# Pinned, delayed transfers, quartered weight loads and a second buffer for the doubles in a fused attention, mixture-of-experts and Fourier-mixing kernel

## The chip, the cores and the metric

The program runs on one core of one Trainium2 chip. The metric is the device time of one execution in microseconds (us); lower is better. A core has five engines that run side by side, each through its own list of instructions in order: TensorE (PE, with PEld for its weight loads), VectorE (DVE), ScalarE (ACT), GpSimd (POOL) and SyncE (SP), which here does little but issue transfers. They wait for each other through semaphores. A transfer is issued by an engine and then carried out by the core's DMA engines.

## The reference

Three stages follow one another for 8 batches of 576 tokens with 512 channels: attention against keys and values that are averaged over 8 tokens, a mixture of 8 experts with a routing that carries over along the tokens, and a Fourier transform over both axes with a normalization and a two-layer network behind it. Cut to what is computed:

```python
def _attn_ref(q, k, v):                        # (8, 8, 576, 64) each
    k_p = k.reshape(B, H, Sp, pool, D).mean(axis=3)          # Sp = 72
    v_p = v.reshape(B, H, Sp, pool, D).mean(axis=3)
    scores = scale * np.matmul(q, k_p.transpose(0, 1, 3, 2))
    scores = scores - np.max(scores, axis=-1, keepdims=True)
    attn = np.exp(scores)
    attn = attn / (np.sum(attn, axis=-1, keepdims=True) + 1e-09)
    return np.matmul(attn, v_p)

def _moe_ref(x, w_gate, w_local, w1, w2):      # w1 (8, 512, 1024), w2 (8, 1024, 512)
    ...                                        # per token: e = fresh argmax, or the token before's
    h = np.maximum(x[b, s] @ w1[e], 0.0)
    out[b, s] = p[e] * (h @ w2[e])

def _moe2_ref(x, w_ch1, w_ch2):                # the weights are doubles
    mixed = np.real(np.fft.fft(np.fft.fft(x, axis=1), axis=2))
    u = x + mixed
    un = (u - mu) / np.sqrt(var + 1e-06)
    return u + np.maximum(un @ w_ch1, 0.0) @ w_ch2
```

## The kernel before

The program has a first part (attention and experts, batch by batch) and a second part (the Fourier mixing and its network), with a loop between them (L1112) that runs once for each further expert that a batch needs; with these data it runs zero times.

**First part.** `moe(b)` multiplies the 576 tokens of batch b by the two weight matrices of one expert, w1 (L460, L461) and w2 (L483, L490). The weights are split into two half-precision parts, so each product is three matmuls. `moe` is a generator of 34 steps. After each step the main loop (L1101 to L1106) advances `chain()`, which runs the attention of the batches to come a fixed number of its own steps further, and `fill()`, which takes a step from `todo`, a list of small jobs. So during moe(b) the program holds the second half of the attention of batch b+1, the first half of that of batch b+2, the load of the weights of b+1 and their splitting, and the decoding of the doubles of the second part.

**One attention tile.** A batch has five tiles. Each goes through `load_q` (L212), `att_A` (L225: PE transposes q), `att_B` (L237: PE scores at L239, softmax on DVE and ACT, the result in two half-precision parts `ehl` at L260 and L261, then a DMA transpose of `ehl` into the tile `ET` at L263), `att_D` (L280: PE multiplies ET by the averaged values at L290, into `xhl`), and `att_L` (PE at L308, the routing). When all five are through, the expert is known, and the program reads its number into a register of SP (L326).

**Weights.** `load_w` (L390) loads one matrix of an expert, 2 MB, in two transfers of 1 MB (L395): w1 into the buffer `wr0`, w2 into `wr1`. In the trace both are `wr`. `max_parts` (L400) takes the largest weight (DVE L405), spreads it over the partitions by an all-reduce on POOL (`across`, L139, tile `wm`), and makes a scale of it (DVE L131). `split_parts` (L422) then makes the two parts: ACT scales (L431) and rounds (L432), POOL subtracts (L433, tiles `w0l` for w1 and `w1l` for w2). `wr0` and `wr1` have one buffer each, so the w2 of batch b+1 can be loaded only after POOL has written the `w1l` of batch b. POOL also averages the keys and values (L170 to L172).

**Doubles.** The weights of the second part come as 64-bit numbers and are decoded in 32 pieces of 512 KB (`load_f64` L620 into the tile `dd`, ACT L635 into `et`, DVE L637 to L641 into `dt`, store at L644). `dd` has one buffer, so each load of a piece waits for the piece before to be decoded (L641).

**What sets the order.** Nearly all transfers are issued by SP, one after the other in SP's list. The program's text gives a first order, but a scheduler of the framework places each instruction by its own priorities; only an instruction marked with `tc.keep_in_program_order` keeps its place in the text. In the first part nothing is so marked before. A transfer that must wait (for its data or for its buffer) holds up every transfer behind it in SP's list.

## Time and profile before

| what | value |
| --- | --- |
| three timed runs | 1580.87, 1561.38, 1581.09 us; median 1580.87 |
| the profiled execution | 1555.29 us |
| its span, from the first to the last instruction | 1553.5 us |
| busy in the span: PE, DVE, ACT, POOL | 1360.3 (88%), 1044.4 (67%), 569.3 (37%), 383.5 us (25%) |
| start, attention of batch 0 | 0 to 76.7 us |
| moe(0) to moe(6) begin on PE at | 76.7, 156.5, 237.7, 322.4, 401.1, 489.1, 565.0 us |
| the last matmul of moe(6) ends | 626.6 us |
| PE waits at the loop | to 647.6 us |
| second part | 647.6 to 1553.5 us |

All times in the rows are of the profiled execution, in us from the start of its span. The profile groups instructions by source line, engine, operation and tiles, written out<-in. A wait in it is the idle time of an engine ahead of an instruction, together with what ended it.

### The profile page before, as it was taken

What the parts mean: (1) busy time and instruction counts of PE and PEld (TensorE: products, weight loads), DVE (VectorE), ACT (ScalarE), POOL (GpSimd) and SP (SyncE); (2) the same over time, 40 slices, a digit from 0 to 9 for tenths busy, and PEclk for the clock granted to TensorE, in tenths of its full rate; (3) what the DMA queues carried; (4) which work ended last, traced back from release to release, by engine and by line L of the source; (5) the groups of instructions that cost most, each with busy time, mean ns of one, the idle gap of its engine ahead of it and who ended that gap; (6) DMA issues with size and microseconds to landing.
All of it is one profiled execution on the core that took longest, in us unless ns stands there. A gap on an engine that the chain in (4) does not pass through costs nothing.

```text
span 1553.5 us, 24994 instructions
## 1 busy us (share of the span) xinstructions
PE 1360.3 (88%) x9674; PEld 842.6 (54%) x9674; DVE 1044.4 (67%) x2197; ACT 569.3 (37%) x1071; POOL 383.5 (25%) x465
## 2 busy tenths in 40 slices
PE   3588888787888898487699999999999999999997
PEld 2454444454444454243566666666666766666663
DVE  5797877776686788258487687565667676576432
ACT  1365556464547475335332221222222221222110
POOL 3562926253446141336201010010101001000000
PEclk8589999898999899679699999999999999999999
DMA  8659897787796767335536053161605235243010
GB/s 164 177 143 254 188 243 178 227 159 236 149 286 163 201 160 194 104 100 147 92 109 131 20 102 62 59 105 49 108 8 113 51 82 82 78 109 75 12 44 28
DMA packets 245954, 193.98 MB, mean 125 GB/s; under 512 B 185254, under 2 KB 191270, under 8 KB 244806
## 3 DMA queue, kind: packets, MB, share of 16 engines
q1 hardware_dynamic: 230198, 172.21, 46.7%
q0 software_dynamic: 10272, 10.41, 2.9%
q10 hardware_dynamic: 5360, 9.70, 1.8%
q8 instruction: 78, 1.28, 0.3%
q14 instruction: 46, 0.38, 0.1%
HBM read 111.83 MB, written 47.37 MB: 102 GB/s over the span
## 4 chain that ended last, share of the span: by engine, by line
PE 47%; DMA 5%; DVE 3%; issue 1%; SPq 1%; ACT 1%; POOL 0%; DVEq 0%; ACTq 0%
PE mm L920 18%; PE s L987 11%; PE et L987 6%; PE hg L987 5%; DMA out_dram<-c 2%; PE mm L460 2%; PE a L870 2%; PE a L869 1%; PE a L877 1%; DMA xhl<-un 1%; DMA dd<-fw_dram 1%; PE a L758 1%; SPq L993 0%; SPq L817 0%; DMA ab<-un 0%
## 5 line engine op out<-in xcount | busy, mean ns | idle before, releaser
L925 DVE TENSOR_TENSOR c<-mm,c 128x512 f32<-128x512 f32 x180 | 122.7, 686 | 151.0 <-PE mm L920 146.4
L460 PE MATMUL mm<-xhl,w0h 128*128 128x512 f16 x512 | 172.9, 406 | 32.9 <-POOLq L1112 21.0
L920 PEld LDWEIGHTS <-wr 128*128 128x128 f16 x1728 | 168.9, 98 | 60.1 <-issue 22.1
L772 POOL DMA_DIRECT2D yb<-y_dram x42 | 26.8, 655 | 475.4 <-DVE pt L822 391.6
L920 PEld LDWEIGHTS <-ex 128*128 128x128 f16 x1296 | 126.8, 99 | 25.3 <-issue 5.1
L987 PEld LDWEIGHTS <-hl 128*128 128x128 f16 x864 | 83.8, 98 | 94.9 <-issue 1.6
L987 PEld LDWEIGHTS <-hh 128*128 128x128 f16 x864 | 84.6, 98 | 86.7 <-issue 0.5
L920 PE MATMUL mm<-xhl,wr 128*128 128x256 f16 x864 | 107.5, 275 | 22.0 <-DMA xhl<-un 22.0
L930 ACT COPY c<-mm 128x512 f32<-128x512 f32 x72 | 41.4, 584 | 185.7 <-PE mm L920 161.4
L920 PE MATMUL mm<-xhl,ex 128*128 128x256 f16 x864 | 108.4, 277 | 0.0
L936 ACT ACTIVATE hl<-c 128x512 f16<-128x512 f32 x72 | 45.3, 629 | 163.2 <-DVE c L925 163.2
L460 PE MATMUL mm<-xhl,w0l 128*128 128x512 f16 x256 | 103.2, 403 | 0.0
L490 PE MATMUL mm<-w1h,hh 128*128 128x512 f16 x256 | 99.7, 389 | 0.5 <-DVE hl L465 0.5
L460 PEld LDWEIGHTS <-w0h 128*128 128x128 f16 x512 | 50.8, 102 | 89.5 <-issue 39.3
L490 PE MATMUL mm<-w1h,hl 128*128 128x512 f16 x256 | 99.0, 387 | 0.0
L490 PE MATMUL mm<-w1l,hh 128*128 128x512 f16 x256 | 98.9, 386 | 0.0
L936 ACT ACTIVATE hh<-c 128x512 f16<-128x512 f32 x72 | 44.9, 630 | 119.2 <-DVE c L925 119.1
L431 ACT ACTIVATE wr<-wr,wscale 128x512 f32<-128x512 f32 x120 | 82.0, 718 | 10.6 <-DVE wscale L135 8.0
L461 PE MATMUL hg<-xhl,w0h 128*128 128x64 f16 x512 | 84.5, 197 | 0.0
L433 POOL TENSOR_TENSOR w0l<-wr,w0h 128x512 f16<-128x512 f32 x56 | 63.3, 1155 | 69.4 <-ACT wr L431 23.0
L405 DVE TENSOR_REDUCE wmax<-wr 128x1 f32<-128x1024 f32 x64 | 76.6, 1210 | 4.2 <-DMA wr<-in_moe_w_dram 4.2
L490 PEld LDWEIGHTS <-hh 128*128 128x128 f16 x512 | 48.9, 99 | 53.4 <-issue 4.2
(296 smaller groups left out, 3138.3 us busy)
## 6 DMA issues: line engine op xcount, KB each, us to landing
wr<-in_moe_w_dram SPq DMA_DIRECT2D x32, 1024.0 KB
dd<-in_moe_w_ch_dram SPq DMA_DIRECT2D x32, 512.0 KB
kraw<-in_k_dram SPq DMA_DIRECT2D x8, 1152.0 KB
vraw<-in_v_dram SPq DMA_DIRECT2D x8, 1152.0 KB
xs_dram<-xhl SPq DMA_DIRECT2D x8, 1152.0 KB
y_dram<-y ACTq DMA_DIRECT2D x32, 256.0 KB
fw_dram<-dt SPq DMA_DIRECT2D x32, 256.0 KB
u_dram<-yb SPq DMA_DIRECT2D x32, 256.0 KB
```

Source lines behind the costliest of these rows:

```text
L405: V.tensor_reduce(out=m[:, c:c + 1], in_=tc_, axis=AX.X, op=ALU.max, apply_absolute_value=True)
L431: S.activation(out=t[:, sl], in_=t[:, sl], func=ACTF.Copy, scale=s)
L433: G.tensor_tensor(out=l[:, sl], in0=t[:, sl], in1=h[:, sl], op=ALU.subtract)
L460: P.matmul(po, lhsT=ww[:, c], rhs=x[:, j, kk, 64:576], start=st, stop=sp)
L461: P.matmul(go, lhsT=ww[:, c], rhs=x[:, j, kk, 0:64], start=st, stop=sp)
L490: P.matmul(po, lhsT=hx[:, f, c0:c0 + n], rhs=ww[:, 512 * f:512 * f + 512], start=(f == 0 and t == 0), stop=(f == 7 and t == 2))
L870: P.matmul(o, lhsT=fd[2][gw, n, :M], rhs=tabs[nm][gw, 1, i], start=False, stop=True)
L920: P.matmul(o[:, q], lhsT=fw1[n][:, w, kk, f], rhs=unT[b][x][:, u, kk, :], start=(kk == 0 and i == 0), stop=(kk == 1 and i == 2))
L925: TT(out=c, in0=x, in1=y, op=ALU.add)
L930: S.copy(out=c, in_=o)
L936: S.activation(out=d[0], in_=c, func=ACTF.Relu)
L987: P.matmul(acc[i], lhsT=h[:, x, hf, q, 128 * i:128 * i + 128], rhs=fw2[w][hf][:, 512 * f:512 * f + 512], start=(f == 0 and hf == 0 and n = ...
```

## The change

It has five pieces, all in the first part.

1. **Transposes.** `att_B` no longer issues the transpose of `ehl` at once. It puts it on a list `later`, which is worked off at the end of the next step of the chain (`do_later`), and the transpose is pinned to that place of the program.
2. **q.** `load_q` within `attention` goes on the same list, and its transfers are pinned.
3. **Weights.** `load_w` becomes a generator of four pinned transfers of 512 KB. `moe` puts the generator on a list `loads`, and `steps` issues one quarter after each step of `moe`.
4. **Doubles.** `dd` has two buffers in the first part. Two pieces are loaded at the start, a piece fetches the one after the next, and its load and its store are pinned and stand one step later.
5. **Housekeeping.** A table of `count_extras` reuses a tile. In the loop (`in_order`) nothing is pinned.

The loads of the keys and values and the read of the expert's number are not pinned.

```diff
-    BUFS = {"xhl": 2, ..., "c": 5}
+    BUFS = {"xhl": 2, ..., "c": 5, "dd": 2}
+    def pin(ins):
+        return ins if in_order else tc.keep_in_program_order(ins)
+    in_order = []
+    later = []
+    def do_later():
+        for f in later:
+            f()
+        later.clear()
@@ load_q
-            D.dma_start(out=t, in_=q[b, :, s0:s0 + 128, :].rearrange("h s d -> s h d"))
+            pin(D.dma_start(out=t, in_=q[b, :, s0:s0 + 128, :].rearrange("h s d -> s h d")))
@@ att_B
-        D.dma_start_transpose(out=ET[b, i][:, :, :, :n]..., in_=hl[:n]...)
+        et = ET[b, i]
+        later.append(lambda: pin(D.dma_start_transpose(out=et[:, :, :, :n]..., in_=hl[:n]...)))
@@ load_w
-        kc = 4 if which == 0 else 8
-        for h in range(2):
-            n = kc // 2
-            D.dma_start(out=tile_[:, 2048 * h:2048 * h + 2048]...,
-                        in_=src[bass.ds(e, 1), 128 * n * h:128 * n * (h + 1)]...)
+        n = (1, 2)[which]
         wr[key, which] = tile_
+        for h in range(4):
+            pin(D.dma_start(out=tile_[:, 1024 * h:1024 * h + 1024]...,
+                            in_=src[bass.ds(e, 1), 128 * n * h:128 * n * (h + 1)]...))
+            yield
@@ moe, beside
-                load_w(b + 1, ereg[b + 1], 0, wtile([128, 4096], F32, "wr0"))
+                loads.append(load_w(b + 1, ereg[b + 1], 0, wtile([128, 4096], F32, "wr0")))
...
-                load_w(b + 1, ereg[b + 1], 1, wtile([128, 4096], F32, "wr1"))
+                loads.append(load_w(b + 1, ereg[b + 1], 1, wtile([128, 4096], F32, "wr1")))
+        def steps(g):
+            for _ in g:
+                if loads and next(loads[0], "end") == "end":
+                    loads.pop(0)
+                yield
-            yield from moe1_f(b, f, hh, hl, hg)
+            yield from steps(moe1_f(b, f, hh, hl, hg))
-            yield from moe2_t(b, i, hh, hl, c, done)
+            yield from steps(moe2_t(b, i, hh, hl, c, done))
+        for g in loads:
+            drain(g)
@@ attention
-                    load_q(b + (r + 3) // 5, (r + 3) % 5)
+                    later.append(lambda: load_q(b + (r + 3) // 5, (r + 3) % 5))
...
                 yield
+                do_later()
@@ decode_parts
-        load_f64(c + 1)
-        yield
-        D.dma_start(out=fw_dram[c // 2, ...], in_=t.bitcast(F32))
+        yield
+        load_f64(c + 2)
+        pin(D.dma_start(out=fw_dram[c // 2, ...], in_=t.bitcast(F32)))
         yield
```

Three places of the order, before and of the change. The first is SP's list in moe(5): ET are the transposed attention weights, made of ehl0 or ehl1 in turn, wr0 and wr1 the buffers for w1 and w2. Before:

```order
L326 TENSOR_LOAD fe_i_5666
L326 ISA x2
L395 ISA
L395 DMA wr0_5724<-in_moe_w1_dram 128x2x1024
L263 DMA_TRANSPOSE ET_5481<-ehl1_99 128x16x128
L395 ISA
L395 DMA wr0_5724<-in_moe_w1_dram 128x2x1024
L395 ISA
L395 DMA wr1_5890<-in_moe_w2_dram 128x4x512
L395 ISA
L395 DMA wr1_5890<-in_moe_w2_dram 128x4x512
L263 DMA_TRANSPOSE ET_5603<-ehl0_98 128x16x128
```

And in the changed kernel (L279 is the transpose, L412 the weight load):

```order
L412 DMA wr0_5750<-in_moe_w1_dram 128x1024
L412 ISA
L412 DMA wr0_5750<-in_moe_w1_dram 128x1024
L279 DMA_TRANSPOSE ET_5629<-ehl0_98 128x16x128
L412 ISA
L412 DMA wr0_5750<-in_moe_w1_dram 128x1024
L279 DMA_TRANSPOSE ET_5802<-ehl1_99 128x16x128
L412 ISA
L412 DMA wr0_5750<-in_moe_w1_dram 128x1024
L412 ISA
L412 DMA wr1_5916<-in_moe_w2_dram 128x2x512
```

The fourth transpose (from ehl0) stood behind all of w1 and both halves of w2; it now stands behind two quarters of w1, and the fifth behind three. The last quarter of w1 stands behind the fifth transpose. In moe(1) to moe(6) of the changed kernel all five transposes stand ahead of the first quarter of wr1.

The second place is POOL's list in moe(4): the all-reduces (L139) of the weights' maxima (wm0 for w1, wm1 for w2) and of the values' (vmax), the averaging (L172) and the splitting (L433). Before:

```order
L139 ISA
L139 ISA wm0_5103<-am_5101 128x1
L139 ISA vmax_5328<-am_5325 128x1
L172 ISA
L172 TENSOR_TENSOR kp_5340<-kraw_5181 72x128
L433 TENSOR_TENSOR w0l_5229<-wr0_4761,w0h_5228 128x512 x3
L139 ISA
L139 ISA wm1_5395<-am_5393 128x1
L433 ISA
L433 TENSOR_TENSOR w0l_5229<-wr0_4761,w0h_5228 128x512 x5
```

And in the changed kernel (L154, L187 and L450 are the same three lines):

```order
L154 ISA
L154 ISA wm0_5129<-am_5127 128x1
L187 ISA
L187 TENSOR_TENSOR kp_5363<-kraw_5207 72x128
L450 TENSOR_TENSOR w0l_5253<-wr0_4783,w0h_5252 128x512 x3
L154 ISA
L154 ISA vmax_5354<-am_5351 128x1
L450 ISA
L450 TENSOR_TENSOR w0l_5253<-wr0_4783,w0h_5252 128x512 x5
L187 TENSOR_TENSOR kp_5363<-kraw_5207 72x128
L154 ISA
L154 ISA wm1_5420<-am_5418 128x1
```

Here two visits to the all-reduce have become three, since vmax no longer goes with wm0. In moe(0) to moe(6) there were 1, 3, 3, 3, 2, 2, 3 visits and are now 2, 2, 3, 2, 3, 2, 3; there are as many in all of the first part.

The third place is PE's list around the last att_D (L290) of moe(3), where a1 is its result and vs are the averaged values. Before:

```order
L461 MATMUL hg_3704<-xhl_2623,w0h_3302 128x64
L460 LDWEIGHTS w0l_3303
L460 MATMUL mm_4149<-xhl_2623,w0l_3303 128x512
L290 LDWEIGHTS vs_3580
L290 MATMUL a1_4097<-ET_3850,vs_3580 64x128
```

And in the changed kernel (L507 is a matmul with w2, L306 is att_D):

```order
L507 MATMUL mm_4220<-w1h_3735,hh_3719 128x512
L507 LDWEIGHTS hh_3719
L507 MATMUL mm_4220<-w1l_3736,hh_3719 128x512
L306 LDWEIGHTS vs_3598
L306 MATMUL a1_4119<-ET_3868,vs_3598 64x128
```

Counted by the wide matmuls (512 columns) of moe(3), the last att_D stood behind 90 of the 96 of the first product, and now stands behind 116, 20 into the second product.

## Rows read from the trace of the kernel before

**Rows 1.** Windows by stage: stretch, length, busy time by engine, PEclk, DMA share, GB/s.

```profile
76.70:565.00 488.30, 411.54 (x3383) 227.36 (x3383) 372.15 (x857) 269.48 (x520) 227.98 (x259) 0.93 0.79 199
626.60:647.60 21.00, 0.04 (x3) 0.02 (x2) 4.77 (x20) 6.99 (x16) 6.34 (x7) 0.56 0.22 67
790.00:1553.50 763.50, 747.79 (x4932) 493.48 (x4929) 484.37 (x940) 180.19 (x318) 39.00 (x68) 1.00 0.32 70
```

**Rows 2.** Waits of PE, 76.7 to 565: us in total, times, longest.

```profile
PE a L290 <- DMA ET<-ehl: 41.6, 14, 8.4
PE mm L460 <- DVE y L506: 7.8, 2, 6.0
```

**Rows 3.** Timeline of PE: start, us, instruction, [idle before <- releaser].

```profile
285.85 1.50 PE L290 MATMUL a<-ET,vs 72*64 72x128 f16 x24 [8.44 <-DMA ET<-ehl]
...
322.36 0.39 PE L460 MATMUL mm<-xhl,w0h 128*128 128x512 f16 x1
...
362.94 1.28 PE L290 MATMUL a<-ET,vs 72*64 72x128 f16 x20 [7.43 <-DMA ET<-ehl]
...
411.97 1.03 PE L460 MATMUL mm<-xhl,w0h 128*128 128x512 f16 x2 [6.01 <-DVE y L506]
...
520.19 1.50 PE L290 MATMUL a<-ET,vs 72*64 72x128 f16 x24 [7.30 <-DMA ET<-ehl]
```

**Rows 4.** Timeline of SP's transfers, around the last stall and one piece of doubles.

```profile
496.39 4.80 SPq L263 DMA_TRANSPOSE ET<-ehl  x1
501.41 9.80 SPq L395 DMA_DIRECT2D wr<-in_moe_w_dram  x3
511.32 6.71 SPq L263 DMA_TRANSPOSE ET<-ehl  x1
...
396.42 0.34 SPq L620 DMA_DIRECT2D dd<-in_moe_w_ch_dram  x1
```

**Rows 5.** Waits of SP's queue, 76.7 to 565.

```profile
SPq L620 <- DVE dt L641: 69.8, 16, 10.2
SPq L263 <- DVE ehl L261: 34.5, 8, 8.2
...
SPq L395 <- POOL w1l L433: 25.8, 5, 7.8
```

**Rows 6.** Windows around the three long stalls, columns as in Rows 1.

```profile
280.80:291.00 10.20, 4.99 (x43) 2.94 (x44) 8.00 (x20) 1.48 (x3) 0.38 (x1) 0.50 1.03 252
359.30:369.50 10.20, 6.57 (x50) 3.48 (x51) 1.45 (x3) 2.32 (x4) 1.60 (x2) 0.50 0.99 287
516.30:526.50 10.20, 6.31 (x52) 3.50 (x53) 4.13 (x9) 1.87 (x3) 0.00 (x0) 0.50 0.65 172
```

**Rows 7.** Waits of ACT for doubles, 76.7 to 565.

```profile
ACT et L635 <- DMA dd<-in_moe_w_ch_dram: 27.2, 13, 5.1
```

**Rows 8.** Timeline of ACT: the decoding of the piece issued at 396.42.

```profile
400.96 0.64 ACT L635 ACTIVATE et<-dd 128x512 f32<-128x512 f32 x1 [2.87 <-DMA dd<-in_moe_w_ch_dram]
```

**Rows 9.** Timeline of POOL: splits and all-reduces.

```profile
314.42 5.60 POOL L433 TENSOR_TENSOR w0l<-wr,w0h 128x512 f16<-128x512 f32 x5 [7.32 <-ACT cm L560]
...
370.10 0.38 POOL L139 PARTITION_ALL_REDUCE wm<-am  x1 [9.12 <-issue]
...
407.86 0.38 POOL L139 PARTITION_ALL_REDUCE wm<-am  x1 [5.97 <-issue]
...
645.99 1.14 POOL L433 TENSOR_TENSOR w1l<-wr,w1h 128x512 f16<-128x512 f32 x1 [7.53 <-issue]
```

**Rows 10.** Timeline of DVE: the fifth tile's ehl and the maximum of w1, moe(3).

```profile
349.09 0.76 DVE L261 TENSOR_TENSOR ehl<-sc,ehl 128x576 f16<-128x576 f32 x1 [1.07 <-ACT ehl L260]
...
357.05 0.15 DVE L147 TENSOR_REDUCE am<-wmax 128x1 f32<-128x4 f32 x1
```

**Rows 11.** Window of two weight halves in flight, columns as in Rows 1.

```profile
348.00:352.00 4.00, 4.00 (x41) 2.18 (x40) 2.73 (x5) 1.65 (x3) 4.00 (x4) 1.00 0.97 394
```

More of the change, by code (lines that the diff above doesn't have):

```diff
@@ L528, in moe @@
         todo.append(w2s)
+        loads = []
         at = {}
@@ L1041, in count_extras @@
     def count_extras():
-        oh = pool["sb"].tile([128, B, 5, 8], F32, tag="x_oh", name="x_oh", bufs=1)
+        oh = mt([128, B, 5, 8], F32, "E")
         cnt = small([128, B, 8], F32, "x_cnt")
@@ L1083, in attention_moe_fourier_kernel @@
         advance(a, done_steps[0] + 1)
-    load_w(0, ereg[0], 0, wtile([128, 4096], F32, "wr0"))
-    load_w(0, ereg[0], 1, wtile([128, 4096], F32, "wr1"))
+    drain(load_w(0, ereg[0], 0, wtile([128, 4096], F32, "wr0")))
+    drain(load_w(0, ereg[0], 1, wtile([128, 4096], F32, "wr1")))
     advance(a, done_steps[0] + WAIT_W)
```

24 lines of the change are left out of this document (13 added, 11 removed).

## The prediction
> **What bounds the kernel now.** I read the windows by stage first. From 790 us on, PE is busy 747.79 of 763.50 us at full clock [rows 1]; the change moves next to nothing there, so that part is taken as it is. In the stretch of moe(0) to moe(5), 76.70 to 565.00, PE is busy 411.54 of 488.30 us, so 76.8 us are lost there, with the DMA engines busy 0.79 of the time. From 626.60 to 647.60 PE does nothing: POOL's last split of w1l begins at 645.99 [rows 1, 9]. That tail waits for POOL's work, which the change leaves as it is.
>
> Next, PE's waits in the first stretch. The largest is att_D's for its transposed weights: 41.6 us in 14 waits [rows 2]. PE's timeline shows that three of them make up more than half: 8.44, 7.43 and 7.30 us, together 23.2 us, ending at 285.85, 362.94 and 520.19 [rows 3]. SP's timeline says why, at the last of them: a transpose at 496.39, then three halves of weights from 501.41 on, which hold SP for 9.80 us, and only at 511.32 the transpose that PE waits for [rows 4]. Among the three halves are those of w2, which wait until POOL has done with w1l: SP waits so 25.8 us in 5 waits, up to 7.8 us each [rows 5]. So the transposes are late because they stand behind loads whose buffer isn't free. The order shows the same in moe(2), moe(3) and moe(5), the three places of the long stalls.
>
> Around each long stall lies a stretch at a granted clock of 0.50, the lower of the two levels (1.2 GHz) [rows 6]. PE is busy there 4.99 + 6.57 + 6.31 = 17.9 us, half of which, 8.9 us, is lost to the clock.
>
> **The change, part by part.**
>
> *Transposes pinned, one step later, and weights in quarters.* These belong together: no transpose stands behind a wr1 quarter of its batch any more, but behind at most three quarters of wr0. And att_D itself stands later on PE (in moe(3) behind 116 wide matmuls rather than 90), so a transpose has more time. I take the three long waits as gone: −23.2 us [rows 3], and with them the low clock: −8.9 us [rows 6]. The eleven shorter waits sum to 41.6 − 23.2 = 18.4 us [rows 2]. Between nothing and all of it I take half, −9.2 us: a transpose still queues behind other data (one held SP 4.80 us with no wait for a buffer [rows 4]), and it is issued a step later.
>
> *Quarters as such.* Two halves in flight together move 394 GB/s, 0.97 of the DMA engines [rows 11]. There are now 24 more transfers in moe(0) to moe(5). Issued at 0.34 us each [rows 4], that is 8 us on SP, which waits 69.8 + 34.5 + 25.8 = 130 us in three lines alone [rows 5]; so I count it as nothing. If SP had no such waits, it would be the 8 us. What a small transfer costs by itself has a bound in the doubles, 512 KB too: issued at 396.42, used at 400.96, 4.5 us [rows 4, 8], against 512 KB / 394 GB/s = 1.3 us in the flow [rows 11]. So it is between 0 and 3.2 us, and since quarters are queued one behind another, I take 0 and keep 3.2 for a rival.
>
> *q.* Its loads were ordered by the scheduler and are now at a fixed place. PE's waits name none of it among the large ones; I take nothing.
>
> *Doubles in two buffers.* SP waits 69.8 us for the buffer in 16 waits [rows 5], and ACT 27.2 us for the data [rows 7]. But PE feels this only where ACT or DVE is late for it. The nearest row is PE's wait for y (L506), 7.8 us in 2 waits, of which 6.01 us at 411.97 [rows 2, 3], 11 us behind a decode that had waited 2.87 us for its data [rows 8]. The bounds are 0 and −7.8; I take −2, since DVE's own length of work there doesn't change.
>
> *What comes next: POOL.* So far the gain is 23.2 + 8.9 + 9.2 + 2 = 43.3 us, 7.2 us for each of six batches. If PE is done sooner, the next moe wants its w0l sooner. Now POOL ends w0l at 314.42 + 5.60 = 320.02, and moe(3) starts at 322.36 [rows 3, 9]: a slack of 2.3 us. POOL pays for every visit to the all-reduce: 5.97 us idle before it at 407.86 and 7.53 us before the next split, at 645.99 [rows 9]. In all there are as many visits as before, but moe(2) and moe(4) have three of them, moe(4) one more than it had. There I let POOL take back what goes beyond the slack: 7.2 − 2.3 = 4.9 us, twice, +9.8 us. The bounds are 0 and the same in all six batches, +29.4.
>
> **The sum** is −43.3 + 9.8 = −33.5 us. It is made against the profiled execution, 1555.29 us. The three runs shown are 25.6, 6.1 and 25.8 above it, 19.2 in the mean, which I add: 1574.5 (their median is 6.4 above that). 1574.5 − 33.5 = 1541.0 us.
>
> **The rivals.**
>
> *POOL takes over in every batch.* For it: the slack of 2.3 us, and the switches of 6 and 7.5 us. Against it: POOL is busy only 227.98 of 488.30 us [rows 1]. Then the gain is 43.3 − 29.4 = 14 us, with 8 to 22 around it: 1552 to 1566.
>
> *All waits go.* The two-buffer decode and the fixed order take all of 41.6 + 8.9 + 7.8 = 58.3 us, and POOL gives nothing back, because its inputs come sooner too: 1516; up to 1528 if a part of the short waits stays.
>
> *Slower: the last quarter of w0.* It is pinned behind the fifth transpose, and so behind the fifth ehl, which in moe(3) is done at 349.09 + 0.76 = 349.85 [rows 10]. A transpose held SP 4.80 to 6.71 us [rows 4], and the quarter lands 1.3 to 4.5 us later: at 356 to 361. The maximum is now complete at 357.05 + 0.15 = 357.2 [rows 10], and POOL's all-reduce follows at 370.10; if its switch of 5.97 us begins only with the data, the maximum could come until 364.1 [rows 9]. From there on, 6.9 us later than now, each us would move w0l and the next moe. To undo the gain (33.5 / 6 = 5.6 us for each batch) and add 27 us in all (4.5 for each), it would have to come 5.6 + 4.5 + 2.3 = 12.4 us later still in every batch; that gives 1574.5 + 27 = 1601. Against it: the quarters start early in a batch, and the bounds above end before 364.1.
>
> *The quarters cost by themselves.* At 3.2 us for each of 24 more transfers, one behind another, that is 77 us; with the gain of 33.5, +43: 1618. Against it, the window with two transfers in flight runs at 0.97 [rows 11], and several are queued most of the time.
> The Trainium skill, page "DMA: Bandwidth & Descriptors", section "Bandwidth", says the same in general: transfers should be batched to at least 1 MiB to come near the peak; and its section "Anatomy of one DMA" puts the fixed cost of a transfer at about 2.0 us. By that page, as an estimate, 24 more would cost 48 us if none overlapped, and 1 MB transfers ought to be left whole. The trace agrees that one 512 KB transfer alone is far from the rate of two large ones, but it shows no serial chain of them.
>
> *Nothing happens.* The order shows that the transposes do move, so this can be only if the short waits grow as the long ones go. It is the lower end of the POOL case.
>
> **How the numbers follow.** Chances: forecast, gain of 22 to 46 (1528 to 1552), 0.50; POOL takes over (1552 to 1566), 0.24; all waits go (1516 to 1528, with the noise of the runs to 1508), 0.15; w0's last quarter, 0.07; cost of the quarters, 0.04. Two per cent, about what a measurement of this kernel can tell from no change, is 31.5 us of 1574.5. The forecast lies almost on this bound, so I divide it, 0.28 faster and 0.22 the same. Faster: 0.28 + 0.15 = 0.43. The same: 0.22 + 0.24 + 0.03 (a mild case of the late quarter) = 0.49. Slower: 0.04 + 0.04 = 0.08. The range goes from 1508, where no wait is left and the runs lie 8 us low, to 1568, the end of the POOL case. The forecast's own range is 1528 to 1552.
>
> **What the profile of the changed kernel would show.** Right: PE's waits of att_D for ET fall from 41.6 to about 9 us with none over 4; no stretch at 0.50 between 237 and 565; SP's transfers in moe(2), moe(3) and moe(5) show the transposes ahead of the wr1 quarters; moe(6) starts near 531 rather than 565; PE still waits about 21 us at the loop. For POOL: a wait of L477 (L460 before) for w0l in moe(3) or moe(5) of about 5 us. Wrong: waits for w0l in all batches (POOL took over); SP held at the last wr0 quarter, and the all-reduce wm later than 13 us after POOL's averaging (the late quarter); DVE's maxima (L405 before) waiting for wr batch by batch (the cost of quarters); or a second part that is not as long as before.

## The result, and the profile after

The change makes the kernel **slower by 1.3%**: 1583.66 us (median of 18 runs, 1575.0 to 1588.07) against 1561.23 us before (18 runs, 1552.59 to 1581.09), a ratio of 1.013 with a 95% interval of 1.0103 to 1.0158. That is within 2%, but on the other side of no change than forecast. The three runs shown before were high: the level of before is 1561, not the 1574.5 on which the forecast stood.

The two profiled spans, 1553.5 and 1575.1 us, differ by 21.6 us, close to the 22.4 us between the medians, so they can be laid side by side.

| stretch | before | after | difference |
| --- | --- | --- | --- |
| start, to moe(0) | 76.7 | 77.5 | +0.8 |
| moe(0) to moe(5) | 488.3 | 505.6 | +17.3 |
| moe(6), to its last matmul | 61.6 | 63.1 | +1.4 |
| PE's wait at the loop | 21.0 | 25.7 | +4.7 |
| second part | 905.9 | 903.3 | -2.6 |

The windows by stage of the changed kernel, with the columns of Rows 1: moe(0) to moe(5), then the tail.

```profile
77.48:583.04 505.56, 421.81 (x3360) 230.24 (x3360) 376.39 (x840) 263.88 (x507) 224.80 (x258) 0.90 0.72 192
...
646.10:671.76 25.66, 0.00 (x0) 0.00 (x0) 5.21 (x26) 11.78 (x23) 3.38 (x5) 0.54 0.11 38
```

Against [rows 1], PE is idle 83.8 us rather than 76.8, and its busy time for about the same work (3360 matmuls in the record, 3383 before) has grown from 411.5 to 421.8, with the mean granted clock down from 0.93 to 0.90. So the 17.3 us are 7 us more of idle time and 10.3 us more of busy time.

PE's waits in the changed kernel, moe(0) to moe(5) (us in total, times, longest):

```profile
PE a L241 <- DVE lg L325: 12.8, 2, 8.0
PE a L365 <- DVE r_f L358: 12.3, 4, 5.8
PE a L306 <- DMA ET<-ehl: 10.9, 11, 2.5
PE a L324 <- DVE xhl L311: 8.0, 3, 6.9
...
PE hg L478 <- POOL w0l L450: 5.8, 6, 2.0
PE mm L477 <- ACT w0h L449: 4.2, 1, 4.2
...
PE mm L477 <- POOL w0l L450: 1.4, 1, 1.4
```

The wait for ET has fallen from 41.6 us [rows 2] to 10.9, with none over 2.5: that part did what it should. But two lines that were not among PE's larger waits before, for the routing on DVE (`lg`, L325, and `r_f`, L358), now hold 25.1 us in six waits. DVE's own waits say why. In the changed kernel:

```profile
DVE wm L146 <- POOL wm L154: 37.7, 10, 9.0
DVE wmax L422 <- DMA wr<-in_moe_w_dram: 32.6, 9, 10.3
```

and in the kernel before, over the same batches:

```profile
DVE wm L131 <- POOL wm L139: 19.8, 8, 5.2
...
DVE wmax L405 <- DMA wr<-in_moe_w_dram: 2.6, 3, 1.7
```

`wm` is the maximum of a weight matrix, spread over the partitions by POOL's all-reduce; L146 (L131 before) is DVE's first instruction of the scale made of it. DVE takes its list in order, so while it waits there, everything behind stands still. One such place, in moe(4), in the timeline of the changed kernel (start, us, instruction, [idle before <- releaser]; by engine: SP, DVE, POOL, PE):

```profile
464.60 1.79 SPq L279 DMA_TRANSPOSE ET<-ehl  x1
466.58 1.65 SPq L412 DMA_DIRECT2D wr<-in_moe_w_dram  x2
...
470.85 1.22 DVE L422 TENSOR_REDUCE wmax<-wr 128x1 f32<-128x1024 f32 x1 [2.32 <-DMA wr<-in_moe_w_dram]
...
472.58 0.15 DVE L162 TENSOR_REDUCE am<-wmax 128x1 f32<-128x4 f32 x1
...
482.86 0.15 DVE L146 TENSOR_SCALAR wm<-wm 128x1 f32<-128x1 f32 x1 [8.99 <-POOL wm L154]
482.93 0.18 DVE L325 TENSOR_REDUCE lg<-a 128x9 f32<-128x27 f32 x1
...
471.76 1.41 POOL L186 TENSOR_TENSOR vraw<-vraw 72x256 f32<-72x256 f32 x2
482.44 0.38 POOL L154 PARTITION_ALL_REDUCE wm<-am  x1 [9.27 <-issue]
...
483.16 1.12 PE L241 MATMUL a<-ident,q 128*128 128x128 f32 x4 [7.99 <-DVE lg L325]
```

Read it from the top. The last quarter of w1 goes out behind the batch's fifth transpose, at 466.6. The maximum is complete on DVE at 472.7. POOL has just finished averaging the values, at 473.2, and is idle for 9.27 us before its all-reduce, at 482.44. DVE's list has two instructions between the maximum and the scale, so DVE stands still for 8.99 us; directly behind the scale is `lg`, and PE waits 7.99 us for it. Four of PE's stalls end like this, 0.3 to 2.5 us after such a scale: 5.82 us at 240.94, 4.82 at 312.34, 3.99 at 404.8 and 7.99 at 483.16, together 22.6 us. The three stalls that the change removed were 23.2 us [rows 3]. Of DVE's 37.7 us at the scale, 28.6 are at that of w1; before, it was 4.7 of 19.8.

Before, DVE did not wait at all for the all-reduce of w1 in five of the seven batches. Here it is in moe(2) of the kernel before, on POOL and DVE:

```profile
286.93 0.38 POOL L139 PARTITION_ALL_REDUCE wm<-am  x1 [11.48 <-DVE am L147]
...
286.65 0.15 DVE L147 TENSOR_REDUCE am<-wmax 128x1 f32<-128x4 f32 x1
...
288.64 0.14 DVE L131 TENSOR_SCALAR wm<-wm 128x1 f32<-128x1 f32 x1
```

POOL had ended its averaging at 275.5, 11 us before the maximum came, and began the all-reduce 0.1 us after it. In the changed kernel the maximum of w1 and the end of POOL's element-wise work ahead of the all-reduce fall within 3.2 us of each other in moe(0) to moe(4), and the all-reduce follows 6.9 to 10.3 us after the maximum.

A second kind of stall has grown. In moe(3) `fe_c`, an instruction of the routing on eight numbers (DVE L338), lasts 7.20 us; in moe(3) of the kernel before it takes 0.21 us. Here are DVE, POOL and PE:

```profile
358.57 7.20 DVE L338 SCALAR_TENSOR_TENSOR fe_c<-lg,fe_m,tab 1x8 f32<-1x8 f32 x1
...
360.15 5.58 POOL L450 TENSOR_TENSOR w1l<-wr,w1h 128x512 f16<-128x512 f32 x5
...
367.44 0.27 PE L324 MATMUL a<-wg_hl,xhl 128*128 128x9 f16 x4 [6.93 <-DVE xhl L311]
```

POOL is busy without a gap from 356.56 to 365.73, and `fe_c` ends at 365.77; PE's second longest stall ends 1.7 us later. In moe(0) `fe_c` lasts 3.76 us, and PE's stall of 3.84 us at 116.91 stands behind it. (The kernel before has one such `fe_c`, 3.28 us at 109.34.) In the 18 traces of this case together, 45 of DVE's small routing instructions (`fe_c`, `r_ss`, `r_m`, `r_oh`, `p_all`, `cm`) last over 2 us, up to 19.05. Each of them lies in a stretch in which POOL does one element-wise instruction after another, and ends within 0.13 us of the end of one of POOL's. So POOL's work seems to hold up DVE without any semaphore. No run tests this.

Each of the four stalls behind the scale brings the low clock back, too. The windows of 8 us behind two of them:

```profile
312.30:320.30 8.00, 7.96 (x32) 3.94 (x33) 5.96 (x19) 6.45 (x13) 1.44 (x2) 0.69 0.47 153
...
483.10:491.10 8.00, 7.94 (x34) 3.95 (x35) 6.03 (x21) 6.43 (x13) 0.97 (x2) 0.70 0.51 145
```

Around the four stalls the granted clock is 0.50, the lower level (1.2 GHz), for 27.2 us, against 30.6 us around the three that went [rows 6]. So with their clock the four cost about what the three had cost: they explain why nothing was won. In all of moe(0) to moe(5), though, the clock is at 0.50 for 100 us rather than 71. Among the parts of the loss on top are the two stalls behind `fe_c`, 10.8 us, a wait of 4.17 us for the first part of w1 at the start of moe(1), and the low clock around these (0.50 for 13.7 us from 109.0, for 10.2 us from 163.6 and for 6.8 us from 365.0).

### The profile page after: what moved, and what is told of

Its sections match the earlier page's. It is cut to its first block, busy times and chain, and to the rows that moved or that the text cites. A ratio compares the mean times of both kernels' runs of the same rounds, so it can differ in the third digit from the quotient of the medians.

```text
span 1575.1 us, 25121 instructions
## 1 busy us (share of the span) xinstructions
PE 1374.6 (87%) x9674; PEld 848.1 (54%) x9674; DVE 1057.2 (67%) x2197; ACT 569.6 (36%) x1071; POOL 381.0 (24%) x465
## 4 chain that ended last, share of the span: by engine, by line
PE 46%; DMA 5%; DVE 2%; SPq 1%; issue 1%; ACT 1%; ACTq 0%; DVEq 0%
PE mm L944 18%; PE s L1011 10%; PE et L1011 6%; PE hg L1011 5%; DMA out_dram<-c 2%; DMA xhl<-un 2%; PE a L894 2%; PE mm L477 2%; PE a L893 1%; PE a L901 1%; DMA dd<-fw_dram 1%; SPq L1017 1%; PE a L786 1%; SPq L841 0%; DVE c L949 0%
## 5 line engine op out<-in xcount | busy, mean ns | idle before, releaser
L477 PE MATMUL mm<-xhl,w0h 128*128 128x512 f16 x512 | 174.7, 412 | 39.8 <-POOLq L1137 25.7
L1011 PEld LDWEIGHTS <-hl 128*128 128x128 f16 x864 | 83.8, 98 | 94.8 <-issue 1.5
L507 PE MATMUL mm<-w1h,hh 128*128 128x512 f16 x256 | 101.2, 395 | 0.8 <-DVE hl L482 0.7
L507 PE MATMUL mm<-w1h,hl 128*128 128x512 f16 x256 | 101.0, 395 | 0.0
L507 PE MATMUL mm<-w1l,hh 128*128 128x512 f16 x256 | 100.9, 394 | 0.0
L422 DVE TENSOR_REDUCE wmax<-wr 128x1 f32<-128x1024 f32 x64 | 76.8, 1203 | 35.4 <-DMA wr<-in_moe_w_dram 35.4
L450 POOL TENSOR_TENSOR w1l<-wr,w1h 128x512 f16<-128x512 f32 x64 | 72.7, 1156 | 42.3 <-ACT w1h L449 13.1
L507 PEld LDWEIGHTS <-hh 128*128 128x128 f16 x512 | 49.5, 101 | 56.4 <-issue 9.9
L450 POOL TENSOR_TENSOR w0l<-wr,w0h 128x512 f16<-128x512 f32 x56 | 62.9, 1147 | 54.6 <-DMA dd<-in_moe_w_ch_dram 10.2
```

What stands on the lines that cost most here:

```text
L422: V.tensor_reduce(out=m[:, c:c + 1], in_=tc_, axis=AX.X, op=ALU.max, apply_absolute_value=True)
L450: G.tensor_tensor(out=l[:, sl], in0=t[:, sl], in1=h[:, sl], op=ALU.subtract)
L477: P.matmul(po, lhsT=ww[:, c], rhs=x[:, j, kk, 64:576], start=st, stop=sp)
L507: P.matmul(po, lhsT=hx[:, f, c0:c0 + n], rhs=ww[:, 512 * f:512 * f + 512], start=(f == 0 and t == 0), stop=(f == 7 and t == 2))
L1011: P.matmul(acc[i], lhsT=h[:, x, hf, q, 128 * i:128 * i + 128], rhs=fw2[w][hf][:, 512 * f:512 * f + 512], start=(f == 0 and hf == 0 and n = ...
```

## The experiments

Times are medians; ratios are against runs of the kernel before on the same chip, with 95% intervals. "The changed kernel" is 1583.66 us throughout.

### Taking the pieces out, one at a time

Theory A, as it stood at first: the last quarter of w1 comes late, behind the fifth transpose, and DVE then stands at the scale. Rivals: the doubles, the clock, the cost of quarters.

**Weights as before**: two halves in place of the quarters, unpinned, both at once rather than one for each step.

```diff
-        for h in range(4):
-            pin(D.dma_start(out=tile_[:, 1024 * h:1024 * h + 1024]..., in_=src...))
-            yield
+        for h in range(2):
+            D.dma_start(out=tile_[:, 2048 * h:2048 * h + 2048]..., in_=src...)
```

> The changed kernel, but with the weights loaded as before: two unpinned halves of 1 MB issued at once. Theory A (the last quarter of w1 stands behind the fifth transpose, so the maximum of w1 is complete late, and DVE stands in order at the scale behind POOL's all-reduce with the routing behind it): the maximum of w1 comes 34 to 54 us after a moe's start again instead of 37 to 72, the four PE stalls of 4.0 to 8.0 us behind DVE's lg and r_f (22.6 us together) go, and the time falls by 20 us or more, to 1540 to 1563 us. Rival B (the doubles' second buffer loads DVE with work at the wrong moment): it stays at 1580 to 1587 us. Rival C (the clock alone): it stays within 5 us of 1583, since the short waits stay.

Measured: 1579.17 us, ratio 1.010 (1.0064 to 1.0135). Theory A missed. The maximum of w1 did come early again (DVE's waits at the maxima are 3.1 us), but PE's waits became these:

```profile
PE a L306 <- DMA ET<-ehl: 54.5, 11, 11.7
PE a L306 <- ACT vs L434: 16.5, 4, 8.8
```

With the transposes delayed and the halves issued at once, a transpose stands directly behind both halves of w2 in every batch, and SP waits 43.0 us for `w1l` ahead of these loads (29.9 before, over the same 70 to 600 us). So this run exchanges one loss for another, and doesn't tell what the quarters cost. It also shows that DVE's stand at the scale isn't a loss of PE in every order: it is 41.0 us here, and PE's waits behind lg and r_f are 0.7 us.

**Doubles as before**: one buffer, nothing pinned.

```diff
-        yield
-        load_f64(c + 2)
-        pin(D.dma_start(out=fw_dram...))
+        load_f64(c + 1)
+        yield
+        D.dma_start(out=fw_dram...)
```

> The changed kernel with the doubles as before: one buffer, unpinned, the next piece fetched one step earlier. Theory A (late last quarter of w1, DVE held at the scale): 1578 to 1590 us, PE stalls behind lg and r_f stay. Rival B (the doubles cost the time): back to 1555 to 1567 us. The prediction's own term for the doubles was 2 us of gain, so 1586.

Measured: 1580.19 us, 1.0075 (1.0032 to 1.0117): the time is as expected of Theory A, but its sign is not. PE's waits for lg and r_f did not stay; they are 3.0 us. DVE still stands 31.0 us at the scale, and PE's waits are in other places (11.4 us for vs, 8.0 for w0l, 6.8 for wscale, which is computed at the scale). Taking back the doubles doesn't bring the time back; which stalls make up the loss changes with the order.

**Transposes and q as before**, at once and not pinned.

```diff
-        later.append(lambda: pin(D.dma_start_transpose(out=et..., in_=hl...)))
+        D.dma_start_transpose(out=et..., in_=hl...)
-                    later.append(lambda: load_q(b + (r + 3) // 5, (r + 3) % 5))
+                    load_q(b + (r + 3) // 5, (r + 3) % 5)
```

> The changed kernel with transposes and loads of q as before: issued at once and unpinned, so that the pinned quarters need not stand behind the fifth transpose. Theory A: the scheduler can put the last quarter of w1 ahead of the transposes, the maximum comes earlier by 5 to 15 us in a batch, and the PE stalls behind lg and r_f shrink to under 8 us together; waits of att_D for ET come back to some extent, 10 to 30 us; 1560 to 1578 us. If quarters as such cost (rival D, a rate below that of halves): DVE's waits at the maxima for wr stay at about 33 us and the time at 1580 or more.

Measured: 1558.91 us, 0.9967 (0.9932 to 1.0002), just under the expected range: the whole loss is gone, but not by the way expected. The maximum of w1 is nearly as late as in the changed kernel (complete at 225.6, 303.1 and 382.6 us, 63.6, 46.7 and 42.5 us into moe(1) to moe(3)), and DVE waits 26.1 us for the weights there (33.0 in the changed kernel over the same 70 to 600 us). What has changed is the wait at the scale:

```profile
DVE wmax L422 <- DMA wr<-in_moe_w_dram: 26.1, 10, 9.9
...
DVE wm L146 <- POOL wm L154: 10.8, 7, 3.4
```

In DVE's list 17 to 18 instructions now lie between w1's maximum and the scale in moe(1) to moe(4), where the changed kernel has 10, 2, 11 and 2. POOL switches as slowly as before; DVE has work meanwhile.

But in the profiled execution only 7.5 us of the gain lie in moe(0) to moe(6), and 12.3 in PE's wait at the loop. There POOL does the last all-reduce of a weight (`wm`) and those for the scales of the decoded doubles (`amr`) in one visit, where the changed kernel, and the one before, go back to a `w0l` in between. POOL's timeline in the changed kernel, and in this run:

```profile
648.26 0.38 POOL L154 PARTITION_ALL_REDUCE wm<-am  x1 [6.29 <-issue]
655.61 1.14 POOL L450 TENSOR_TENSOR w0l<-wr,w0h 128x512 f16<-128x512 f32 x1 [6.96 <-ACT wr L448]
662.56 0.72 POOL L154 PARTITION_ALL_REDUCE amr<-am  x2 [5.82 <-issue]
...
640.08 0.38 POOL L154 PARTITION_ALL_REDUCE wm<-am  x1 [5.91 <-DVE et L665]
640.37 0.42 POOL L154 PARTITION_ALL_REDUCE amr<-am  x1
```

**Only the transposes as before** (q still delayed and pinned).

```diff
-        later.append(lambda: pin(D.dma_start_transpose(out=et..., in_=hl...)))
+        D.dma_start_transpose(out=et..., in_=hl...)
```

> The changed kernel, with the transposes issued at once again instead of a step later (pinned or not makes no difference: the order of every engine is the same); q still delayed. In its order DVE has 18 or 19 instructions between w1's maximum and the scale in moe(1), moe(3) and moe(4), where the changed kernel has 10, 11 and 2. Theory A2 (the delay of the transposes shifts DVE's order so that it stands at the scale while POOL switches to the all-reduce): DVE's waits for wm fall from 37.7 to under 18 us and the time to 1553 to 1566 us. Rival Q (the delay of q does it): 1576 us or more.

Measured: 1561.5 us, 1.0019 (0.9994 to 1.0045). So the delay of the transposes is what makes the difference, not q. DVE's waits for wm are 24.1 us, above the 18 expected, and here too most of the gain is POOL's single visit in the tail: PE's wait at the loop is 13.8 us shorter, moe(0) to moe(6) 6.3. The order shows that pinning plays no part: with undelayed transposes the list of every engine is the same, pinned or not.

### Is it DVE's stand at the scale?

**More room ahead of the scale.**

```diff
         r = absmax(m, 128, f"wm{which}")
-        yield
+        for _ in range(5):
+            yield
         inv, s = small([128, 1], F32, f"winv{which}"), ...
```

> The changed kernel with five more steps between POOL's all-reduce of a weight's maximum and the scale made of it on DVE, so that DVE has 14 to 19 other instructions in between for w1 instead of 2. Theory A: DVE's waits for wm (37.7 us between 70 and 600) fall below 15, PE's four stalls behind DVE (22.6 us) to under 8 us together; but the split of w1 comes a few us later, so that PE may wait for w0l instead: 1562 to 1578 us. Rivals B, C, D: no change, 1580 to 1588 us, or slower through the later split.

Measured: 1556.32 us, 0.9959 (0.9922 to 0.9995), 27 us less than the changed kernel and 6 below the expected range, by an edit that adds no work and takes none away (but moves the order on the other engines as well). DVE's waits, and then PE's:

```profile
DVE wm L146 <- POOL wm L154: 15.0, 8, 5.6
...
PE a L306 <- DMA ET<-ehl: 28.6, 15, 5.8
PE a L365 <- DVE r_f L358: 10.3, 2, 8.0
```

The scale waits fell from 37.7 to 15.0 us, where under 15 were expected. One stall behind DVE of 8.0 us remained (10.3 us rather than under 8), and waits for ET came up to 28.6, yet the stretch moe(0) to moe(5) is 481.1 us, 7 less than before the change. Only 2.9 us of the gain are in the tail.

**No all-reduce of the weights' maxima.**

```diff
-        r = absmax(m, 128, f"wm{which}")
+        r = small([128, 1], F32, f"wm{which}")
+        V.tensor_reduce(out=r, in_=m, axis=AX.X, op=ALU.max, apply_absolute_value=True)
```

> The changed kernel without the all-reduce of the weights' maxima: each partition makes its scale of its own maximum, so the part of the computation that is left out is the spreading of the maximum over the partitions, and the products come out with wrong scales. No DVE instruction waits for POOL at the scale any more. Theory A2: PE's stalls behind lg and r_f (25.5 us) shrink to under 8 us, and the time falls by 20 to 40 us, to 1543 to 1563 us. Rival E (the later place of att_D on PE and the late transposes cost the time, whatever DVE waits for): 1572 us or more.

Measured: 1537.51 us, 0.9883 (0.9819 to 0.9946), 46 us less than the changed kernel, more than the 20 to 40 expected. PE's waits for lg are gone, and of those for r_f 1.8 us are left:

```profile
PE a L306 <- DMA ET<-ehl: 25.6, 22, 3.5
...
PE a L365 <- DVE r_f L358: 1.8, 1, 1.8
```

The maximum of w1 is as late as ever (complete 74.6 us into moe(0) and 56.7 into moe(1), against 72.0 and 63.6 in the changed kernel). So its being late costs little where DVE doesn't wait for POOL behind it.

**The mean by PE instead of the maximum by POOL**, in the changed kernel and in the kernel before; `mean` is a matrix of 128x128 times 1/128:

```diff
-        r = absmax(m, 128, f"wm{which}")
+        am, r = small([128, 1], BF16, "wam"), small([128, 1], F32, f"wm{which}")
+        V.tensor_reduce(out=am, in_=m, axis=AX.X, op=ALU.max, apply_absolute_value=True)
         yield
+        pm = bank([128, 1], "a1")
+        P.matmul(pm, lhsT=mean, rhs=am, start=True, stop=True)
+        V.tensor_copy(out=r, in_=pm)
+        yield
```

> The changed kernel with another way to spread the weights' maxima: instead of POOL's all-reduce, PE multiplies the 128 maxima by a matrix of 1/128, which gives every partition their mean (the true maximum is between that and 128 times that; only its power of two is used). DVE then waits for PE instead of POOL, and POOL has no switch for it. Theory A2 (the change loses its gain to DVE standing at the scale during POOL's switch): near the run without the all-reduce, 1535 to 1552 us, faster than the kernel before by 0.5 to 1.5%. Rival: PE, in order, waits for DVE's maximum at the small matmul and loses what was won: 1560 us or more.

> The kernel before with the same replacement of the all-reduce. Theory A2: in the kernel before the switch was mostly hidden (in five of seven batches the all-reduce of w1 came 0.1 to 0.4 us after its maximum), so there is less to win: 1543 to 1558 us, and the changed kernel with the same replacement is faster than this one by 5 to 20 us, since the gain at the transposes then shows. Rival G (the all-reduce costs both alike): 1515 to 1530 us, and the change would stay slower by 1%.

Measured: 1543.99 us, 0.9927 (0.9898 to 0.9956), with the change, and 1550.9 us, 0.9953 (0.9926 to 0.9981), without it. So replacing the all-reduce saves the changed kernel 40 us and the kernel before 10, and with it out of the way the change **gains** 7 us. That is the forecast's direction, at a fifth of its size.

### The pieces alone on the kernel before

> The kernel before with the quartered, pinned weight loads alone (transposes, q and doubles as before). Theory A2: quarters cost nothing by themselves, and the wait of a wr1 load for POOL no longer stands ahead of a transpose: the long stalls for ET (23.2 us) shrink by half or more, DVE's order keeps 16 to 20 instructions ahead of the scale, and the time is 1540 to 1560 us. Rival D (quarters cost by themselves): 1570 us or more, with DVE's waits at the maxima for wr at 30 us or more.

> The kernel before with the delayed transposes and delayed q alone. Theory A2 (the delay shifts DVE's order to its harm, the halves still stand ahead of transposes): 1570 to 1590 us, with waits of att_D for ET of 40 to 60 us as in the run with both the delay and the halves (54.5), and DVE's waits at the scale over 30. If the delay only costs together with the other pieces: 1558 to 1566 us.

> The kernel before with two buffers for the doubles alone, their loads and stores pinned. The prediction's term is a gain of 2 us (0 to 7.8): 1553 to 1562 us, with ACT's waits for dd down from 27 to under 8 us. Theory A2: the same, unless DVE's order moves; there the order has 1 instruction between w1's maximum and the scale in five batches, so if POOL has not switched in time, DVE's waits at the scale go over 35 us and the time to 1570 or more.

> The kernel before with five more steps between the all-reduce of a weight's maximum and the scale on DVE. Theory A2: the stall of 6.01 us at 411.97, which the prediction put down to the decoding, is DVE standing at the scale of wm (408.27, 5.23 us); it goes, the three long stalls for ET stay, and the time falls by 3 to 12 us, to 1550 to 1560 us. If the stall was the decoding: no change, 1558 to 1566 us.

| on the kernel before | us | ratio | moe(0) to moe(5) | PE's wait at the loop |
| --- | --- | --- | --- | --- |
| nothing | 1561.23 | 1 | 488.3 | 21.0 |
| quarters alone | 1586.27 | 1.0158 (1.0092 to 1.0224) | 511.7 | 21.2 |
| delayed transposes and q alone | 1594.22 | 1.0242 (1.0219 to 1.0265) | 521.9 | 20.0 |
| doubles in two buffers alone | 1561.81 | 1.002 (0.9985 to 1.0054) | 513.5 | 11.7 |
| more room ahead of the scale | 1580.94 | 1.0115 (1.005 to 1.018) | 494.2 | 35.4 |

Only the doubles came out as expected in time, and by a trade: in the profiled execution the stretch of the moes is 25 us longer, the tail 9 us and the second part 7 us shorter. The longer stretch is two `fe_c` of 19.05 and 12.10 us beside POOL's work, with PE's stalls of 18.43 and 10.63 us behind them (189.06 and 280.05); the shorter tail is one visit of POOL rather than two. ACT's waits for dd are 11.6 us, not under 8. Quarters alone were expected to gain and lost 25 us; DVE's waits for wm are 24.6 us there, those for the weights 26.9. The time is that of rival D; what speaks against D is that runs with the same quarters are as fast as the kernel before (1558.91) and faster (1540.51 and 1530.8, below). One of its stalls, 9.09 us at 367.76, stands behind an `fe_c` of 9.75 us; the rest of its loss stays open. The delay alone lost more than expected, and not at the scale (DVE's waits for wm are 16.0 us). Its longest stall, 10.51 us at 441.43, stands behind an instruction of DVE of 11.46 us beside POOL's work (`vs`, at 425.53). Its tiles are late at every station:

```profile
PE a L306 <- DMA ET<-ehl: 31.1, 9, 9.4
PE sc L254 <- DVE ehl L276: 23.4, 7, 10.5
PE a L324 <- DVE xhl L311: 14.3, 7, 5.5
```

The fourth edit, the same that helped the changed kernel by 27 us, cost the kernel before 20; DVE's waits at the scale rose from 19.8 to 30.1 us. More than half of that loss is in the tail, where POOL's list now goes to and fro once more (POOL's timeline of that kernel):

```profile
653.11 0.38 POOL L139 PARTITION_ALL_REDUCE amr<-am  x1 [5.77 <-issue]
660.63 1.14 POOL L434 TENSOR_TENSOR w1l<-wr,w1h 128x512 f16<-128x512 f32 x1 [7.14 <-issue]
667.61 0.38 POOL L139 PARTITION_ALL_REDUCE amr<-am  x1 [5.84 <-issue]
674.96 1.14 POOL L434 TENSOR_TENSOR w1l<-wr,w1h 128x512 f16<-128x512 f32 x1 [6.97 <-issue]
```

In the kernel before the two `amr` stand together; here a w1l stands between them, which costs 5.84 + 6.97 = 12.8 us of the 14.4 by which the tail grew.

### The late maximum, and the delay by itself

What was still open: whether the late maximum of w1 costs anything, and whether the delay does so beyond the scale.

**w1's quarters at once** (w2's still one for each step).

```diff
-                loads.append(load_w(b + 1, ereg[b + 1], 0, wtile([128, 4096], F32, "wr0")))
+                drain(load_w(b + 1, ereg[b + 1], 0, wtile([128, 4096], F32, "wr0")))
```

> The changed kernel with the four quarters of w1 issued at once instead of one after each step of moe; all else, the all-reduce and the delay too, as in the changed kernel. The rival of the prediction (the last quarter of w1, late behind the fifth transpose, moves the next moe): the maximum of w1 comes 10 to 20 us earlier in a batch and the time falls to 1555 to 1568 us. Theory A2 (what counts is where DVE's list has the scale; in the order of this kernel it stands 1, 11, 12, 19, 2 and 1 instructions behind the maximum): the maximum comes earlier, but the time stays at 1570 us or more.

Measured: 1540.51 us, 0.9847 (0.9745 to 0.995), 43 us less than the changed kernel. Both expectations missed, the first by its size and the second by its direction. In moe(2), moe(3) and moe(5) all four quarters now stand ahead of the fourth and fifth transposes; the maximum of w1 is complete 33.1 to 53.9 us into moe(0), moe(2) to moe(5), and 27.7 into moe(1), where the changed kernel has 37.5 to 72.0. Of the gain in the profiled execution, 14.7 us are PE's wait at the loop, with POOL's single visit in the tail, and 28 are in moe(0) to moe(6). DVE's waits:

```profile
DVE wmax L422 <- DMA wr<-in_moe_w_dram: 22.4, 8, 4.5
DVE wm L146 <- POOL wm L154: 20.0, 8, 6.5
```

**The same with PE in place of the all-reduce, and the undelayed transposes with PE.**

> The changed kernel with w1's quarters issued at once and with the weights' maxima spread by PE. DVE's waits at the maxima for wr (37.9 us in the run with PE alone) fall below 15 us. If these waits reach PE: 1528 to 1540 us. If they are hidden: 1540 to 1550 us, like the run with PE alone.

> The changed kernel with the transposes issued at once and with the weights' maxima spread by PE instead of POOL's all-reduce. Theory A2 in full (the delay costs only because DVE then stands at the scale during POOL's switch): with the switch gone the delay costs nothing, so this lies within 8 us of the 1544 us of the same kernel with the delay: 1536 to 1552 us. Theory A3 (the delay also costs by itself, through the longer chain of a tile): faster than 1536 us.

Measured: 1551.65 us, 0.9918 (0.9875 to 0.9961), for early quarters with PE, 11 us *more* than with the all-reduce. And 1530.8 us, 0.9752 (0.9652 to 0.9851), for undelayed transposes with PE: 13 us less than with the delay, and the fastest kernel of this study (1.9% ahead of the kernel before by the medians on its chip, 2.5% by the ratio above). But the moes are not what the delay costs there: moe(0) to moe(6) are 531.1 us without it and 531.0 with it. PE's wait at the loop is 9.0 rather than 19.7 us, since POOL does the all-reduces `amr` ahead of all of `w1l`, and with the delay only behind three of its eight parts.

**Early quarters and undelayed transposes.**

> The changed kernel with w1's quarters issued at once and the transposes issued at once. Theory A3 (the delay costs some 13 us by itself, as between the runs with PE, beside what it costs through the late maximum): 1522 to 1533 us. Theory A2 (it costs only through the late maximum, which the early quarters have already mended): 1535 to 1548 us, like the run with early quarters and the delay (1540.5). If two such remedies get in each other's way, as early quarters and PE did (1551.7): over 1548 us.

Measured: 1560.12 us, 0.9999 (0.9967 to 1.0031), the third of the expectations: 20 us more than with the delay. So the delay isn't bad by itself in every order, and these gains don't add. Two things are visible in the trace: POOL has its two visits in the tail again (22.5 us at the loop, where the run with the delay has 11.0), and an instruction of the routing (`r_m`) lasts 11.52 us beside POOL's work, with PE's stall of 10.60 us at 236.70 behind it.

### What is shown and what stays open

Two stretches of the profiled executions, in us, tell the effects on the moes from those on the tail:

| kernel | moe(0) to moe(6) | PE's wait at the loop |
| --- | --- | --- |
| before | 549.9 | 21.0 |
| changed | 568.6 | 25.7 |
| changed, transposes and q as before | 561.1 | 13.3 |
| changed, only the transposes as before | 562.3 | 11.9 |
| changed, more room ahead of the scale | 549.2 | 22.8 |
| changed, no all-reduce of the weights' maxima | 525.7 | 19.5 |
| changed, mean by PE | 531.0 | 19.7 |
| before, mean by PE | 542.2 | 19.5 |
| changed, w1's quarters at once | 540.4 | 11.0 |

In the three kernels without the all-reduce of the weights the start, up to moe(0), is 6 to 7 us longer.

Shown: in the changed kernel, four of PE's new stalls (22.6 us) end behind DVE's scale, and DVE there waits for POOL's switch to the all-reduce (timeline). With the all-reduce of the weights out of the way, the moes take 38 to 43 us less in the changed kernel and 8 less in the kernel before. More room ahead of the scale, an edit that leaves the all-reduce as it is, brings the moes back to where they were before the change. Undoing the weights or the doubles does not. Undoing the delay gives back 6 to 8 us of the 19 there; the larger part of its gain is in the tail. In all traces with the all-reduce of the weights, PE's wait at the loop is 11.0 to 13.3 us where `amr` follows directly on `wm`, 19.7 to 25.7 where POOL goes back to its splitting once in between, and 35.4 where it does so twice.

Not shown is that the scale makes all of the loss. Each of these edits moves the order on all engines, so none takes away one wait alone, and the same edit helps in one order and harms in another: the extra room gained 27 us and lost 20, PE's mean gained 40, 31 and 10 us and lost 11, the delay cost 22 and 13 us and gained 20. How much of the 22.4 us is the scale, how much `fe_c` beside POOL and how much the low clock around each was not separated. What in the scheduler's choice decides between the orders wasn't tried and stays open.

## Why the prediction was wrong

**The long stalls: right.** 41.6 us of waits for ET became 10.9, where 32.4 us of gain were put in the sum. The order of SP's list was the right thing to read.

**The clock: wrong.** 8.9 us were to come back. PE's busy time grew by 10.3 us: the four stalls behind the scale bring as much time at 0.50 as the three had that went (27.2 and 30.6 us), and others came besides. A term for the clock holds only if the stall isn't replaced.

**The doubles: near in size by luck, their place wrong.** ACT's waits for dd fell from 27.2 us [rows 7] to 5.1, and by themselves the two buffers brought no difference (1561.81), but by a loss in the moes and gains behind them that nearly cancel. But the row that bounded this term, 6.01 us for y at 411.97 [rows 2, 3], had another cause. DVE stood at the scale just ahead of it:

```profile
408.27 0.15 DVE L131 TENSOR_SCALAR wm<-wm 128x1 f32<-128x1 f32 x1 [5.23 <-POOL wm L139]
```

That row of before held the mechanism, and the prediction read past it to a decode 11 us earlier.

**POOL gives back 9.8 us: the right engine, the wrong victim.** This is the step that failed: the sum set against its 43.3 us of gain only PE's wait for w0l, and nothing for DVE. PE's waits for w0l are 7.2 us, near the 9.8 of the sum, though none is over 2.0 where about 5 was foreseen. But the prediction asked only who needs the *result* of POOL's work, and not who stands *behind* the instruction that waits for it. DVE's scale waits, and behind it in DVE's list are the routing, the scores and xhl of the attention. That wait grew from 19.8 to 37.7 us (at w1's scale from 4.7 to 28.6), and PE's stalls of 22.6 us are its price, with 27.2 us at the low clock around them. That takes back what the three long stalls had given. The sum also had nothing for DVE's instructions that are held beside POOL's work, 10.8 us of PE's stalls. And it counted POOL's visits, of which there are as many as before, and not when they begin: the prediction's own row has 9.12 us of idle time ahead of the all-reduce at 370.10 [rows 9], with DVE's stand of 3.49 us behind it.

**The slower rival: the right event, the wrong price.** The prediction named the last quarter of w1 (its "w0", after the buffer `wr0`) behind the fifth transpose, and gave it 0.07 since its own bounds had the quarter in time. The bounds were made from SP's 4.80 to 6.71 us at a transpose [rows 4]; they left out that a transpose waits for its ehl in SP's list, 83.6 us in 12 waits in the changed kernel, where it was 34.5 in 8 [rows 5]. The maximum of w1 came 20 us later in moe(3) (55.1 us into it rather than 34.8), past the 6.9 us from which the rival was to count. Its price was put on w0l alone. Issuing the quarters at once took 43 us off, by way of the moes and the tail; but without the all-reduce a maximum as late costs little, so its price seems to go through DVE's wait for POOL. Of the prediction's signs, the one for this rival (the all-reduce over 13 us after POOL's averaging) did not come; it came 7.8 to 10.1 us after, in moe(0) to moe(4).

**The quarters as such: right to count nothing.** The run with w1's quarters at once has the same 512 KB transfers and is 1.5% faster than the kernel before. The rule of the Trainium skill that the prediction weighed is to batch transfers to at least 1 MiB ("DMA: Bandwidth & Descriptors", section "Bandwidth"). No run here shows a cost of the smaller size by itself, and this one speaks against it. The fixed cost of about 2.0 us that the prediction takes from the same page of the Trainium skill is given there, in section "Anatomy of one DMA", for transfers that GpSimd issues; the quarters are issued by SP. The quarters alone on the kernel before lost 25 us, for a reason that was not found in full. DVE's waits at the maxima, the prediction's sign for such a cost, did rise from 2.6 to 32.6 us, since the quarters go out one for each step and behind transposes. But these waits aren't the loss: the fastest run has 48.3 us of them.

**The tail: wrong.** It was to stay at 21 us and is 25.7: the maximum of w1 of the last batch is complete 40.4 us into moe(6) rather than 34.5, and POOL's list behind it, the same as before, starts later. It was taken as POOL's work; the runs show that it is mostly POOL's switching, and that another order of the same work makes it 11.0 to 35.4 us.

**The level: wrong by 13 us.** Three runs, two of them at 1581, were taken as the level; 18 runs give 1561. The sum's 33.5 us of gain would have meant 1528 on that level.

## What to carry to other kernels

When a change makes a wait shorter on one engine, look in the new order for every instruction that waits for a slow neighbour (here DVE's scale behind POOL's all-reduce), count what stands between it and the instruction that feeds it, and read what is queued behind it: in moe(1) to moe(4), with 2 to 11 instructions in between DVE stood 4.0 to 9.0 us at a time, with 17 or 18 at most 2.3. A transfer that is moved behind others takes on their waits for data, not only their time in the queue. And where a scheduler places the instructions, time a piece of a change together with the others: alone on the kernel before, two of these pieces cost more than all of them together. Compare stretch by stretch as well: two edits with the same total can have gained in the moes or in the tail.

## What the runs showed of the hardware

POOL needs some time to go between its element-wise work and the all-reduce, and it can do so while it waits for the data: 11 us after its last averaging the all-reduce followed the maximum within 0.3 us (286.93 in the kernel before), directly behind it only after 9.27 idle us (482.44 in the changed kernel). To and fro in a tail without other work it is 5.84 us there and 6.97 us back. I had counted the number of these visits, which the change leaves alike, and not whether they are paid in the open.

An instruction of DVE on a few numbers can be held for as long as POOL does element-wise work without a gap: 0.21 us (333.9 in the kernel before) became 7.20 us beside POOL's work (358.57 in the changed kernel), and 19.05 us in the run with the doubles alone, over 23 of POOL's instructions. It shows as a long instruction and not as a wait, so no list of waits names it.
